# TensorE's queue kept in the order of the source from the third group on, and attention two slots sooner

## The chip, the cores and the metric

The kernel runs on one core of a Trainium2 chip. The metric is the time of one execution on the device, in microseconds; shown is the median of three runs. One further execution was recorded by the hardware profiler, and all rows below come from it.

## What is computed

Three layers in a row, all with fp32 inputs and outputs: a gated linear attention, a gated feed-forward layer, and a layer of eight experts of which each token uses one.

```python
# attention: 4 sequences, 8 heads, 768 steps, head size 48
for t in range(S):
    state = alpha[:, :, t, :, None] * state + einsum('bhd,bhe->bhde', k[:, :, t], v[:, :, t])
    y[:, :, t] = einsum('bhd,bhde->bhe', q[:, :, t], state)
# feed-forward: 3072 tokens, 384 -> 1536 -> 384
xn = x / sqrt(mean(x * x, -1) + 1e-6) * rms_g
x = (silu(xn @ w_gate) * (xn @ w_val)) @ w_out
# experts: 8 of 384 -> 1024 -> 384, one for each token
e = argmax(x @ r_gate)
out = prob[e] * sigmoid(x @ r_ogate)[e] * (relu(x @ w1[e]) @ w2[e])
```

## The kernel before

**Tiles and groups.** The 3072 tokens are worked in 24 tiles of 128. Attention goes tile by tile, in chunks of a sequence; tiles 0 to 17 take the first three sequences in turn, tiles 18 to 23 the last one. The feed-forward layer takes three tiles at a time: a group, g = 0 to 7, of 384 tokens.

**Feed-forward.** The inner size 1536 is cut into 12 blocks j. For each block there are three slots: ps_g (nine matmuls with w_gate, line 595), ps_v (nine with w_val), and ps_o (nine with w_out, line 629, for the block before). Each is three matmuls of high and low parts for three pieces of the sum or three tiles. These are the large matmuls: 128 rows, 128 columns of weights, 384 or 400 columns streamed, in the type fp32r. Groups 0 and 1 run first in halves, as the weights still arrive: run s = 0 is group 0 with blocks 0 to 5, s = 1 is group 1 with the same blocks, s = 2 and 3 are the two groups with blocks 6 to 11. Groups 2 to 7 follow, each with all 12 blocks. The experts come behind group 7.

**Attention.** Each tile has five stages on TensorE, in plain fp32, which lie between the slots of an earlier group:
- ps_s (line 416): the scores, eight small matmuls. Their operands have 48 rows each, heads of even number in rows 0 to 47 and of odd number in rows 64 to 111. VectorE masks them into P.
- ps_k (436): k transposed. The last tile of a sequence has none.
- ps_y (447 and 451): q times the running state (the tile "wide", all 128 rows and columns; the first tile of a sequence has none), then P times v, with 64 columns of weights.
- ps_st (472): the addition to the state.
- ps_x (493): the result transposed. It becomes xh and xl, which the next group's ps_g reads.

The stages of group 2's tiles (6, 7 and 8) lie in the runs s = 2 and 3, and those of group g + 1 in group g. VectorE makes qT and kT ahead (lines 315 and 397).

**What sets the order.** The program issues a slot and then, when the function due says so, a stage. A scheduler of the language, which goes by a timing model of its own, then orders the instructions of each engine, and may move one ahead of others that stand before it in the source. The call keep_in_program_order pins an instruction behind everything issued before it on its engine; it is used in a few places by name (the function pace and the tables K0, K1 and K2). Each engine takes its queue strictly in the resulting order.

Of the kernel before, what the change touches and what calls it, by code (L numbers as in the profile page):

```python
# [42 lines left out]
    'RB': 9,  # L43
    'LEADG': 6,
    'NAT': 5,
    'PET': 8,
    'NO': 'arkq',
}
# [4 lines left out]
def gla_glu_moe_kernel(  # L53
# [16 lines left out]
    nc = tc.nc  # L70
    P = 128
    B, H, S, D = q.shape
# [4 lines left out]
    KD = DM // P  # L77
# [5 lines left out]
    GT = 3  # L83
# [77 lines left out]
    def weight(nm, j):  # L161

        end = j >= JM
        if (nm, end) not in wts:
            n = KF - JM if end else JM
            wts[nm, end] = wpool.tile([P, n, WO] if nm[1] == "o" else [P, KD, n * P], F32R,
                                      tag=nm + "e" * end, name=nm + "e" * end)
        t_ = wts[nm, end]
        j -= JM * end
        return t_[:, j, :] if nm[1] == "o" else t_[:, :, j * P:j * P + P]  # L170
# [33 lines left out]
    xT = {}  # L204
    SEATS = CFG['SEATS']
    spread = [True]
    junk = [psM.tile([P, 4, P], F32, tag='o2', name='junk')]
    paced = [CFG['K0']]

# [191 lines left out]
    def stages(t):  # L401
        b, c = place_of[t]
        first, final = c == 0, c == NCH - 1
        en, qT, kT = pre[t]
        Sc = state_of[b % BS]
        S_ = wide[0]
        rs = [slice(64 * hh, 64 * hh + D) for hh in range(2)]
        g, ti = divmod(t, GT)
        Pt = {}

        def score():
            ps = [bank([P, NP, P], "ps_s") for _ in range(2)]
            for p in range(NP):
                for hh in range(2):
                    r = slice(64 * hh, 64 * hh + D)
                    nc.tensor.matmul(ps[hh][:, p, :], lhsT=kT[r, p, :], rhs=qT[r, p, :], start=True, stop=True)  # L416

            def post():
                if not first:
                    nc.vector.tensor_tensor(out=Sc, in0=Sc, in1=en.to_broadcast([P, NP, D]), op=ALU.mult)  # L420
                    for hh in range(2):
                        nc.scalar.activation(S_[rs[hh], :, hh * D:hh * D + D], Sc[rs[hh]], AF.Copy)
                mb = mask.to_broadcast([P, NP, P])
                for hh in range(2):
                    Ph = seat_of(t, f"P{hh}", [P, NP, P])
                    pace(f'Ph{t}', nc.vector.tensor_tensor(out=Ph, in0=ps[hh], in1=mb, op=ALU.mult))
                    Pt[hh] = Ph
            return post
        yield score

        def ktr():
            if final:
                return None
            ps = bank([P, NP, P], "ps_k")
            for p in range(NP):
                nc.tensor.transpose(ps[:, p, :], kT[:, p, :], ident)  # L436
            kn = seat_of(t, "kn", [P, H, 64])
            nc.scalar.activation(kn, ps.rearrange("p a (h d) -> p (a h) d", h=2), AF.Copy)
            Pt["kn"] = kn
            return None  # L440
        yield ktr

        def outp():
            ps = bank([P, DM], "ps_y")
            if not first:
                for p in range(NP):
                    nc.tensor.matmul(ps[:, p * 2 * D:p * 2 * D + 2 * D], lhsT=qT[:, p, :], rhs=S_[:, p, :],  # L447
                                     start=(p == 0), stop=False, skip_group_check=True)
            for h in (0, 2, 4, 6, 1, 3, 5, 7):
                for u in (slice(0, 64), slice(64, P)):  # L450
                    nc.tensor.matmul(ps[u, h * D:h * D + D], lhsT=Pt[h % 2][:, h // 2, u], rhs=vt[t][:, h, :],  # L451
                                     start=first, stop=True, skip_group_check=True)

            def post():
                xn = seat_of(t, "xn", [P, DM])
                ss = att.tile([P, 1], F32, tag="ss", name="ss", bufs=2)
                pace(f'xs{t}', nc.scalar.activation(xn, ps, AF.Square, accum_out=ss))  # L457
                nc.gpsimd.tensor_scalar(out=ss, in0=ss, scalar1=1.0 / DM, scalar2=1e-6, op0=ALU.mult, op1=ALU.add)  # L458
                pace(f'ss{t}', nc.gpsimd.tensor_tensor(out=ss, in0=ss, in1=mhalf, op=ALU.pow))
                pace(f'xa{t}', nc.scalar.activation(xn, ps, AF.Copy, scale=ss[:, 0:1]))  # L460
                Pt["xn"] = xn
            return post
        yield outp

        def state():
            if final:
                return None
            kn = Pt["kn"]
            ps = bank([P, NP, D], "ps_st")
            for p in range(NP):  # L470
                for hh in range(2):
                    nc.tensor.matmul(ps[64 * hh:64 * hh + 64, p, :], lhsT=kn[:, 2 * p + hh, :],  # L472
                                     rhs=vt[t][:, 2 * p + hh, :], start=True, stop=True)

            def post():
                if first:
                    nc.scalar.activation(Sc, ps, AF.Copy)
                else:
                    nc.vector.tensor_tensor(out=Sc, in0=ps, in1=Sc, op=ALU.add)
            return post  # L480
        yield state

        def xtr():
            if t and t + 2 < NTILE:
                load_v(t + 2)
            if ti == 0:
                xT[g] = (act.tile([P, KD, G], F32R, tag="xh", name="xh"),
                         act.tile([P, KD, G], F32R, tag="xl", name="xl"))
            xh, xl = xT[g]
            xn = Pt["xn"]  # L490
            ps = bank([P, KD, P], "ps_x")
            for kc in range(KD):
                nc.tensor.transpose(ps[:, kc, :], xn[:, kc * P:kc * P + P], ident)  # L493
            sl = slice(ti * P, ti * P + P)

            def post():
                xf = xn.rearrange("p (a b) -> p a b", a=KD)
                for kc in range(KD):
                    pace(f'xg{t}', nc.scalar.activation(xf[:, kc, :], ps[:, kc, :], AF.Copy, scale=gT[:, kc:kc + 1]))
                pace(f'xh{t}', nc.scalar.activation(xh[:, :, sl], xf, AF.Copy))  # L500
                pace(f'xl{t}', nc.vector.tensor_tensor(out=xl[:, :, sl], in0=xf, in1=f(xh[:, :, sl]), op=ALU.subtract))
            return post
        yield xtr
# [87 lines left out]
    def mm3(ps, wh, wl, xh, xl):  # L591
        n = 0
        for kc in range(KD):
            for a_, b_ in ((wh, xh), (wh, xl), (wl, xh)):
                nc.tensor.matmul(ps, lhsT=a_[:, kc, :], rhs=b_[:, kc, :],  # L595
                                 start=(n == 0), stop=(n == 3 * KD - 1))
                n += 1

    def m_val(g, j):
# [21 lines left out]
    def m_out(s, j):  # L621
        g, j0, j1 = runs[s]
        if j == j0:
            obank[s] = [psM.tile([P, WO], F32, tag=f"o{i}", name="ps_o") for i in range(GT)]
        hh, hl, _ = hbuf.pop((g, j))
        for i in range(GT):
            sl = slice(i * P, i * P + P)
            for n, (a_, b_) in enumerate(((hh, "woh"), (hh, "wol"), (hl, "woh"))):
                nc.tensor.matmul(obank[s][i], lhsT=a_[:, sl], rhs=weight(b_, j),  # L629
                                 start=(j == j0 and n == 0), stop=(j == j1 - 1 and n == 2))  # L630

    rows = {}

# [55 lines left out]
    def route_b(g):  # L689
        oh, ohb, ohc, m8, og, se = rt.pop(g)  # L690
        R = rows[g]
        ps = psR[0].tile([P, GT + 1, E], F32, tag=psR[1], name="ps_r")
        nc.tensor.matmul(ps[:, 0:1, :], lhsT=tri_b, rhs=ohb[:, 0:1, :], start=True, stop=True)
        for i in range(1, GT):
            nc.tensor.matmul(ps[:, i, :], lhsT=tri_b, rhs=ohb[:, i, :], start=True, stop=False)
            nc.tensor.matmul(ps[:, i, :], lhsT=ones_b, rhs=ohc[:, i - 1, :], start=False, stop=True)
        nc.tensor.matmul(ps[:, GT, :], lhsT=ones_b, rhs=ohc[:, GT - 1, :], start=True, stop=True)
        bc = [P, GT, E]

        nc.vector.tensor_scalar(out=se, in0=se, scalar1=1e-9, scalar2=2.0, op0=ALU.add, op1=ALU.mult)  # L700
# [151 lines left out]
    def due(s, n):  # L852

        if s == 0:
            return done < GS and (n + 1 - AHEAD) * GS >= (done + 1) * (N - AHEAD - CFG['TS'])
        k_ = done - GS
        return (n + 1 + N * (s - 2)) * GS >= (k_ + 1) * 2 * N and k_ < GS and (k_ < NST - 1 or s >= CFG['XG'])

    for s in range(4):
        N = 3 * (runs[s][2] - runs[s][1])  # L860
        paced[0] = CFG['K2'] if s else CFG['K1']
        for n in range(N):
# [193 lines left out]

    for g in range(2, NG):
        last = g == NG - 1
        if last:
            psA.release()  # L1060
            att.release()
# [285 lines left out]
```

## Time and profile before

| | |
|---|---|
| median of three runs | 876.1 us (875.66 to 876.71) |
| profiled execution, its time | 880.26 us |
| its span on the core | 878.6 us |
| TensorE, matmuls | 856.1 us busy, 97% |
| TensorE, weight loads | 814.5 us busy, 93% |
| VectorE | 489.3 us busy, 56% |
| ScalarE | 326.0 us busy, 37% |
| GpSimd | 143.8 us busy, 16% |
| mean granted clock of TensorE | 0.99 |

The busy time of matmuls overlaps, since one starts before the one ahead has ended, so it says that TensorE is never idle, and not how fast it works. A matmul in fp32 leaves two records in the trace for one of the source, one in fp32r a single one.

### The profile page before, as it was taken

To read this page: it belongs to the slowest core of one execution; us is meant where nothing else is said; L and a number is where in the kernel's file an instruction comes from. 1 tells how busy PE (TensorE), PEld (TensorE's weight loads), DVE (VectorE), ACT (ScalarE), POOL (GpSimd) and SP (SyncE) were. 2 spreads that over 40 slices of the span, in tenths; PEclk is the share of its full clock that TensorE was granted. 3 is DMA by queue.
4 is the path that set the end of the run, shared out by engine and by line. 5 is a ranking of instruction groups with operands and counts; after the bars stand their busy time and mean duration, and the time that the engine had idled before them with its cause. 6 is when DMAs were issued, how large, how long until landed. Compare 5 with 4: busy or idle time off the path is not lost.

```text
span 878.6 us, 15655 instructions
## 1 busy us (share of the span) xinstructions
PE 856.1 (97%) x6042; PEld 814.5 (93%) x6042; DVE 489.3 (56%) x1108; ACT 326.0 (37%) x708; POOL 143.8 (16%) x204
## 2 busy tenths in 40 slices
PE   7999999999999999999999999999999999999994
PEld 6799999899999999999999999999988999999994
DVE  7899987576854656655665552244454443444330
ACT  1655554234333233332322333334234442445431
POOL 2001001001100100010010010013032343344331
PEclk8999999999999999999999999999999999999998
DMA  9855534493311222132231010023056164256510
GB/s 190 181 163 149 175 83 122 117 258 89 104 49 36 78 57 61 43 87 60 59 87 47 13 37 1 1 93 98 1 182 197 60 212 144 65 190 198 178 41 24
DMA packets 121660, 88.46 MB, mean 101 GB/s; under 512 B 58219, under 2 KB 116716, under 8 KB 121584
## 3 DMA queue, kind: packets, MB, share of 16 engines
q1 hardware_dynamic: 117120, 77.97, 33.4%
q0 software_dynamic: 4464, 9.48, 3.1%
q8 instruction: 48, 0.79, 0.4%
q14 instruction: 28, 0.23, 0.1%
HBM read 71.62 MB, written 16.07 MB: 100 GB/s over the span
## 4 chain that ended last, share of the span: by engine, by line
PE 85%; DMA 5%; issue 4%; DVE 2%; POOL 1%; ACT 1%; SPq 1%; POOLq 0%; DVEq 0%; ACTq 0%
PE ps_o L629 18%; PE ps_v L595 18%; PE ps_g L595 18%; PE ps_b L1037 8%; PE ps_h L595 7%; PE ps_s L416 4%; PE ps_y L451 3%; DMA st<-in_moe_w_dram 3%; PE ps_y L447 2%; DMA er<-bucket 1%; PE ps_st L472 1%; PE ps_k L436 1%; PE ps_x L493 1%; POOL out_dram L1053 1%; PE pc L560 1%
## 5 line engine op out<-in xcount | busy, mean ns | idle before, releaser
L606 DVE TENSOR_TENSOR tt<-tt,ps_v 128x384 f32<-128x384 f32 x96 | 52.8, 550 | 140.9 <-PE ps_v L595 136.5
L587 ACT ACTIVATE tt<-ps_g 128x384 f32<-128x384 f32 x96 | 47.0, 490 | 135.4 <-PE ps_g L595 132.3
L609 ACT ACTIVATE hh<-tt 128x384 fp32r<-128x384 f32 x96 | 50.2, 523 | 119.6 <-DVE tt L606 119.2
L615 DVE TENSOR_TENSOR hl<-tt,hh 128x384 fp32r<-128x384 f32 x96 | 54.4, 567 | 28.1 <-ACT hh L609 27.4
L1037 PE MATMUL ps_b<-w2a,h 128*128 128x384 f32 (+2 forms) x336 | 67.4, 339 | 1.1 <-ACT h L1021 1.1
L595 PE MATMUL ps_g<-xh,wgh 128*128 128x384 f32 x192 | 68.1, 355 | 0.0
L595 PE MATMUL ps_v<-xh,wvh 128*128 128x384 f32 x192 | 68.0, 354 | 0.0
L1022 DVE SCALAR_TENSOR_TENSOR h<-ps_h,h 128x256 fp32r<-128x256 f32 (+6 forms) x72 | 38.0, 531 | 52.3 <-ACT h L1021 52.0
L629 PE MATMUL ps_o<-wol,hh 128*128 128x400 f32 x192 | 66.6, 347 | 0.0
L629 PE MATMUL ps_o<-woh,hh 128*128 128x400 f32 x192 | 66.5, 353 | 0.0
L1037 PE MATMUL ps_b<-w2b,h 128*114 128x384 f32 (+3 forms) x336 | 65.0, 338 | 0.2 <-ACT h L1021 0.2
L595 PE MATMUL ps_g<-xh,wgl 128*128 128x384 f32 x192 | 65.1, 339 | 0.0
L595 PE MATMUL ps_v<-xh,wvl 128*128 128x384 f32 x192 | 65.0, 339 | 0.0
L595 PE MATMUL ps_g<-xl,wgh 128*128 128x384 f32 x192 | 64.9, 338 | 0.0
L629 PE MATMUL ps_o<-woh,hl 128*128 128x400 f32 x192 | 64.7, 346 | 0.0
L595 PE MATMUL ps_v<-xl,wvh 128*128 128x384 f32 x192 | 64.7, 337 | 0.0
L1037 PEld LDWEIGHTS ps_b<-w2a,h 128*128 128x128 f32 (+2 forms) x336 | 57.5, 181 | 2.6 <-ACT h L1021 2.0
L1037 PEld LDWEIGHTS ps_b<-w2b,h 128*114 128x114 f32 (+3 forms) x336 | 57.5, 175 | 2.1 <-ACT h L1021 0.6
L595 PE MATMUL ps_h<-x,w1b 128*128 128x456 f32 (+3 forms) x288 | 58.5, 344 | 0.3 <-DVE h L1022 0.2
L1021 ACT ACTIVATE h<-ps_h 128x256 fp32r<-128x256 f32 (+6 forms) x72 | 33.3, 467 | 64.8 <-PE ps_h L595 60.4
L595 PE MATMUL ps_h<-x,w1a 128*128 128x256 f32 (+3 forms) x288 | 53.5, 328 | 0.6 <-DVE h L1022 0.6
L458 POOL TENSOR_SCALAR ss<-ss 128x1 f32<-128x1 f32 x24 | 6.4, 266 | 281.0 <-ACT xn L457 276.1
(284 smaller groups left out, 1994.9 us busy)
## 6 DMA issues: line engine op xcount, KB each, us to landing
st<-in_moe_w_dram SPq DMA_DIRECT2D x64, 384.0 KB, 5.4
bucket<-zero SPq DMA_DIRECT2D x8, 772.0 KB, 6.2
stg<-in_moe_w_gate_dram SPq DMA_DIRECT2D x12, 384.0 KB, 3.9
stg<-in_moe_w_val_dram SPq DMA_DIRECT2D x12, 384.0 KB, 3.7
stg<-in_moe_w_out_dram SPq DMA_DIRECT2D x12, 384.0 KB, 3.0
v<-in_v_dram SPq DMA_DIRECT2D x23, 192.0 KB, 2.8
blk_a<-in_alpha_dram SPq DMA_DIRECT2D x32, 96.0 KB, 2.2
blk_k<-in_k_dram SPq DMA_DIRECT2D x32, 96.0 KB, 2.3
```

What stands on the lines that cost most here:

```text
L416: nc.tensor.matmul(ps[hh][:, p, :], lhsT=kT[r, p, :], rhs=qT[r, p, :], start=True, stop=True)
L447: nc.tensor.matmul(ps[:, p * 2 * D:p * 2 * D + 2 * D], lhsT=qT[:, p, :], rhs=S_[:, p, :], start=(p == 0), stop=False, skip_group_check=True)
L451: nc.tensor.matmul(ps[u, h * D:h * D + D], lhsT=Pt[h % 2][:, h // 2, u], rhs=vt[t][:, h, :], start=first, stop=True, skip_group_check=True)
L587: nc.scalar.activation(tt, ps, AF.Silu)
L595: nc.tensor.matmul(ps, lhsT=a_[:, kc, :], rhs=b_[:, kc, :], start=(n == 0), stop=(n == 3 * KD - 1))
L606: nc.vector.tensor_tensor(out=tt, in0=tt, in1=ps, op=ALU.mult)
L609: nc.scalar.activation(hh, tt, AF.Copy)
L615: nc.vector.tensor_tensor(out=hl, in0=tt, in1=f(hh), op=ALU.subtract)
L629: nc.tensor.matmul(obank[s][i], lhsT=a_[:, sl], rhs=weight(b_, j), start=(j == j0 and n == 0), stop=(j == j1 - 1 and n == 2))
L1021: nc.scalar.activation(hh[:, 0, :], ps, AF.Relu)
L1022: nc.vector.scalar_tensor_tensor(out=hh[:, 1, :], in0=ps, scalar=0.0, in1=f(hh[:, 0, :]), op0=ALU.max, op1=ALU.subtract)
L1037: ins = nc.tensor.matmul(ob2[u][i][0:r], lhsT=hh[:, a_, sl], rhs=we[p][b_][:, j, :], start=(j == 0 and m == 0), stop=(j == KF2 - 1 and m = ...
```

## The change

A switch named strict is added. While it is set, a new function seq pins TensorE's instructions of the feed-forward layer, of the five stages and of the routing in the order of the source. It is off in the four half runs (the number STRICT is 4, and s is 0 to 3), on for the groups 2 to 6, and off for the last. Beside this the number XO moves the condition for the stages of tiles 6 to 8 by two slots.

```diff
+    'XO': 2,
+    'STRICT': 4,
...
+    strict = [False]
+
+    def seq(ins):
+
+        if strict[0]:
+            tc.keep_in_program_order(ins)
...
-                    nc.tensor.matmul(ps[hh][:, p, :], lhsT=kT[r, p, :], rhs=qT[r, p, :], start=True, stop=True)
+                    seq(nc.tensor.matmul(ps[hh][:, p, :], lhsT=kT[r, p, :], rhs=qT[r, p, :], start=True, stop=True))
...
-        return (n + 1 + N * (s - 2)) * GS >= (k_ + 1) * 2 * N and k_ < GS and (k_ < NST - 1 or s >= CFG['XG'])
+        return (n + 1 + CFG['XO'] + N * (s - 2)) * GS >= (k_ + 1) * 2 * N and k_ < GS and (k_ < NST - 1 or s >= CFG['XG'])
 
     for s in range(4):
+        strict[0] = s >= CFG['STRICT']
...
     for g in range(2, NG):
         last = g == NG - 1
+        strict[0] = g + 2 >= CFG['STRICT'] and not last
```

The matmuls and transpositions of ps_k, ps_y, ps_st, ps_x, ps_g, ps_v, ps_o and of the routing (ps_r) are wrapped in seq in the same way.

TensorE's queue at the scores of tile 11, in group 2, before; the rows left out are the rest of nine ps_g, of nine ps_v and of nine ps_o:

```order
L493 MATMUL ps_x<-ident,xn 128x128 x3
...
L595 MATMUL ps_g<-xh,wgl 128x384
L416 MATMUL ps_s<-qT,kT 128x128
L595 MATMUL ps_v<-xh,wvh 128x384
...
L629 MATMUL ps_o<-woh,hl 128x400
L416 MATMUL ps_s<-qT,kT 128x128 x7
L595 MATMUL ps_g<-xh,wgh 128x384
```

And now, with the lines of the changed source, which are 9 or so higher:

```order
L502 MATMUL ps_x<-ident,xn 128x128 x3
...
L604 MATMUL ps_g<-xh,wgl 128x384
L604 MATMUL ps_v<-xh,wvh 128x384
...
L638 MATMUL ps_o<-woh,hl 128x400
L425 MATMUL ps_s<-qT,kT 128x128 x8
L604 MATMUL ps_g<-xh,wgh 128x384
```

The first of the eight score matmuls has gone from its place behind ps_g to the other seven. Twelve more of the tiles 11 to 23 differ in the same way, three of them with two matmuls in the first piece and one with two early pieces.

TensorE's queue at the scores of tile 8, in the run s = 3, before:

```order
L493 MATMUL ps_x<-ident,xn 128x128 x3
L595 MATMUL ps_g<-xh,wgle 128x384
L595 MATMUL ps_v<-xh,wvhe 128x384
...
L629 MATMUL ps_o<-wol,hh 128x400
L416 MATMUL ps_s<-qT,kT 128x128 x2
L629 MATMUL ps_o<-woh,hl 128x400 x3
L416 MATMUL ps_s<-qT,kT 128x128 x6
L595 MATMUL ps_g<-xh,wghe 128x384
```

And now:

```order
L502 MATMUL ps_x<-ident,xn 128x128 x3
L604 MATMUL ps_g<-xh,wgle 128x384
L425 MATMUL ps_s<-qT,kT 128x128 x8
L604 MATMUL ps_v<-xh,wvhe 128x384
...
L638 MATMUL ps_o<-woh,hl 128x400
L445 MATMUL ps_k<-ident,kT 128x128 x4
L604 MATMUL ps_g<-xh,wghe 128x384
```

All eight now stand ahead of the nine ps_v, and the transposition of k, which came after the next ps_g and ps_v, ahead of that ps_g.

TensorE's queue at ps_y of tile 18, the first of the last sequence, before; the rows left out are nine ps_g and nine ps_v:

```order
L451 MATMUL ps_y<-v,P_4829 64x48
L595 MATMUL ps_g<-xh,wgh 128x384
...
L451 MATMUL ps_y<-v,P_4829 64x48
L595 MATMUL ps_v<-xh,wvh 128x384
...
L451 MATMUL ps_y<-v,P_4829 64x48 x6
L451 MATMUL ps_y<-v,P_4831 64x48 x8
L629 MATMUL ps_o<-wohe,hh 128x400
```

And now:

```order
L638 MATMUL ps_o<-wohe,hl 128x400
L604 MATMUL ps_g<-xh,wgh 128x384
...
L604 MATMUL ps_v<-xh,wvl 128x384
L460 MATMUL ps_y<-v,P_4829 64x48 x8
L460 MATMUL ps_y<-v,P_4831 64x48 x8
L638 MATMUL ps_o<-wohe,hh 128x400
```

The two early matmuls have joined the others behind ps_v.

## Rows read from the trace of the kernel before

**Rows 1.** Busy time of each engine in two stretches (us; records in brackets).
```profile
core 0: us, PE busy (x) PEld busy (x) DVE busy (x) ACT busy (x) POOL busy (x), PEclk, DMA share, GB/s
200.00:550.00 350.00, 350.00 (x2640) 331.45 (x2638) 201.92 (x480) 113.79 (x272) 31.13 (x59) 1.00 0.22 56
550.00:860.00 310.00, 307.14 (x1839) 298.83 (x1839) 126.40 (x259) 121.17 (x222) 94.63 (x65) 1.00 0.37 118
```

**Rows 2.** TensorE in order of time, first piece of tile 11: start, duration.
```profile
241.30 0.34 PE L595 MATMUL ps_g<-xh,wgh 128*128 128x384 f32 x1
...
242.18 0.34 PE L595 MATMUL ps_g<-xh,wgl 128*128 128x384 f32 x1
242.45 0.48 PE L416 MATMUL ps_s<-qT,kT 48*128 48x128 f32 x2
...
243.14 0.34 PE L595 MATMUL ps_v<-xl,wvh 128*128 128x384 f32 x1
```

**Rows 3.** The same view, the second piece of tile 11.
```profile
245.84 0.35 PE L629 MATMUL ps_o<-wol,hh 128*128 128x400 f32 x1
246.03 0.34 PE L629 MATMUL ps_o<-woh,hl 128*128 128x400 f32 x1
246.30 1.16 PE L416 MATMUL ps_s<-qT,kT 48*128 48x128 f32 x14
...
247.67 0.34 PE L595 MATMUL ps_g<-xl,wgh 128*128 128x384 f32 x1
```

**Rows 4.** The same view, the two pieces of tile 13.
```profile
291.90 0.49 PE L416 MATMUL ps_s<-qT,kT 48*128 48x128 f32 x4
...
292.60 0.34 PE L595 MATMUL ps_v<-xl,wvh 128*128 128x384 f32 x1
...
295.76 0.94 PE L416 MATMUL ps_s<-qT,kT 48*128 48x128 f32 x12
...
296.91 0.34 PE L595 MATMUL ps_g<-xl,wgh 128*128 128x384 f32 x1
```

**Rows 5.** The same view, tile 10, whose scores stand whole, with ps_r behind.
```profile
222.67 0.34 PE L595 MATMUL ps_g<-xh,wgl 128*128 128x384 f32 x1
222.94 1.16 PE L416 MATMUL ps_s<-qT,kT 48*128 48x128 f32 x16
224.04 0.18 PE L693 MATMUL ps_r<-ohb,tri_b 128*128 128x8 bf16 x1
...
224.20 0.42 PE L595 MATMUL ps_v<-xh,wvh 128*128 128x384 f32 x1
224.46 0.34 PE L595 MATMUL ps_v<-xl,wvh 128*128 128x384 f32 x1
```

**Rows 6.** Waits of the weight loads, 205 to 560 us: total, times, longest.
```profile
PEld ps_s L416 <- issue: 7.0, 28, 0.3
```

**Rows 7.** TensorE in order of time, two pieces of ps_y with the state.
```profile
190.55 0.34 PE L595 MATMUL ps_g<-xh,wgle 128*128 128x384 f32 x1
190.72 0.36 PE L447 MATMUL ps_y<-wide,qT 128*128 128x96 f32 x2
...
191.12 0.33 PE L595 MATMUL ps_v<-xl,wvhe 128*128 128x384 f32 x1
...
303.80 0.58 PE L447 MATMUL ps_y<-wide,qT 128*128 128x96 f32 x4
...
304.42 0.34 PE L595 MATMUL ps_v<-xl,wvh 128*128 128x384 f32 x1
```

**Rows 8.** The same view, ps_y of tile 18.
```profile
424.88 0.32 PE L451 MATMUL ps_y<-v,P 128*64 128x48 f32 x2
...
425.41 0.34 PE L595 MATMUL ps_v<-xl,wvh 128*128 128x384 f32 x1
...
426.91 1.02 PE L451 MATMUL ps_y<-v,P 128*64 128x48 f32 x28
```

**Rows 9.** VectorE in order of time: masks of tile 8, qT of tile 10.
```profile
186.03 1.26 DVE L426 TENSOR_TENSOR P<-ps_s,mask 128x512 f32<-128x512 f32 x2
...
218.66 0.69 DVE L397 TENSOR_TENSOR qT<-qT,aT 128x512 f32<-128x512 f32 x1
```

More of the change, by code (lines that the diff above doesn't have):

```diff
@@ L435, in ktr @@
             for p in range(NP):
-                nc.tensor.transpose(ps[:, p, :], kT[:, p, :], ident)
+                seq(nc.tensor.transpose(ps[:, p, :], kT[:, p, :], ident))
             kn = seat_of(t, "kn", [P, H, 64])
@@ L446, in outp @@
                 for p in range(NP):
-                    nc.tensor.matmul(ps[:, p * 2 * D:p * 2 * D + 2 * D], lhsT=qT[:, p, :], rhs=S_[:, p, :],
-                                     start=(p == 0), stop=False, skip_group_check=True)
+                    seq(nc.tensor.matmul(ps[:, p * 2 * D:p * 2 * D + 2 * D], lhsT=qT[:, p, :], rhs=S_[:, p, :],
+                                     start=(p == 0), stop=False, skip_group_check=True))
             for h in (0, 2, 4, 6, 1, 3, 5, 7):
                 for u in (slice(0, 64), slice(64, P)):
-                    nc.tensor.matmul(ps[u, h * D:h * D + D], lhsT=Pt[h % 2][:, h // 2, u], rhs=vt[t][:, h, :],
-                                     start=first, stop=True, skip_group_check=True)
+                    seq(nc.tensor.matmul(ps[u, h * D:h * D + D], lhsT=Pt[h % 2][:, h // 2, u], rhs=vt[t][:, h, :],
+                                     start=first, stop=True, skip_group_check=True))
             def post():
@@ L471, in state @@
                 for hh in range(2):
-                    nc.tensor.matmul(ps[64 * hh:64 * hh + 64, p, :], lhsT=kn[:, 2 * p + hh, :],
-                                     rhs=vt[t][:, 2 * p + hh, :], start=True, stop=True)
+                    seq(nc.tensor.matmul(ps[64 * hh:64 * hh + 64, p, :], lhsT=kn[:, 2 * p + hh, :],
+                                     rhs=vt[t][:, 2 * p + hh, :], start=True, stop=True))
             def post():
@@ L492, in xtr @@
             for kc in range(KD):
-                nc.tensor.transpose(ps[:, kc, :], xn[:, kc * P:kc * P + P], ident)
+                seq(nc.tensor.transpose(ps[:, kc, :], xn[:, kc * P:kc * P + P], ident))
             sl = slice(ti * P, ti * P + P)
@@ L594, in mm3 @@
             for a_, b_ in ((wh, xh), (wh, xl), (wl, xh)):
-                nc.tensor.matmul(ps, lhsT=a_[:, kc, :], rhs=b_[:, kc, :],
-                                 start=(n == 0), stop=(n == 3 * KD - 1))
+                seq(nc.tensor.matmul(ps, lhsT=a_[:, kc, :], rhs=b_[:, kc, :],
+                                 start=(n == 0), stop=(n == 3 * KD - 1)))
                 n += 1
@@ L628, in m_out @@
             for n, (a_, b_) in enumerate(((hh, "woh"), (hh, "wol"), (hl, "woh"))):
-                nc.tensor.matmul(obank[s][i], lhsT=a_[:, sl], rhs=weight(b_, j),
-                                 start=(j == j0 and n == 0), stop=(j == j1 - 1 and n == 2))
+                seq(nc.tensor.matmul(obank[s][i], lhsT=a_[:, sl], rhs=weight(b_, j),
+                                 start=(j == j0 and n == 0), stop=(j == j1 - 1 and n == 2)))
     rows = {}
@@ L692, in route_b @@
         ps = psR[0].tile([P, GT + 1, E], F32, tag=psR[1], name="ps_r")
-        nc.tensor.matmul(ps[:, 0:1, :], lhsT=tri_b, rhs=ohb[:, 0:1, :], start=True, stop=True)
+        seq(nc.tensor.matmul(ps[:, 0:1, :], lhsT=tri_b, rhs=ohb[:, 0:1, :], start=True, stop=True))
         for i in range(1, GT):
-            nc.tensor.matmul(ps[:, i, :], lhsT=tri_b, rhs=ohb[:, i, :], start=True, stop=False)
-            nc.tensor.matmul(ps[:, i, :], lhsT=ones_b, rhs=ohc[:, i - 1, :], start=False, stop=True)
-        nc.tensor.matmul(ps[:, GT, :], lhsT=ones_b, rhs=ohc[:, GT - 1, :], start=True, stop=True)
+            seq(nc.tensor.matmul(ps[:, i, :], lhsT=tri_b, rhs=ohb[:, i, :], start=True, stop=False))
+            seq(nc.tensor.matmul(ps[:, i, :], lhsT=ones_b, rhs=ohc[:, i - 1, :], start=False, stop=True))
+        seq(nc.tensor.matmul(ps[:, GT, :], lhsT=ones_b, rhs=ohc[:, GT - 1, :], start=True, stop=True))
         bc = [P, GT, E]
```

## Prediction

> **What bounds the kernel now.** I first read the busy time of the engines by stretch [rows 1]. From 200 to 550 us TensorE shows 350.00 us of matmul in 350 us, and the list of waits of its matmuls is empty from 205 to 560 us; VectorE has 202 us of work and ScalarE 114. From 550 to 860 us TensorE is still at 307 of 310. So this kernel lasts as long as TensorE's queue takes to run through, and only two things can move it: how much time the instructions of that queue take in the array, and gaps between them. A busy figure of 100% hides the first, because the end of a matmul is modelled and matmuls overlap. What counts is the distance from one start to the next, so the second view is the order of time on TensorE alone, read by starts.
>
> There the large matmuls of the feed-forward part follow each other very evenly: five intervals from 241.30 to 242.18, 0.176 us each [rows 2]; ps_o, with 400 columns, takes 0.19 [rows 3]. Between them lie the small groups of attention. The price of a group is the start of the last large matmul ahead of it to the start of the second one behind it, less two ordinary intervals. (The first one behind starts early enough but holds the next one up, so it must be inside.) An fp32 matmul of the source leaves two records, so the x8 of a ps_s in the program is x16 in the trace.
>
> The price of ps_s, whose operands have 48 of 128 rows:
> - one matmul alone (x2): 242.18 to 243.14 is 0.96, less 0.35: 0.61 us [rows 2]
> - two alone (x4): 291.90 to 292.60 is 0.70, with the same 0.27 ahead of it, less 0.35: 0.62 us [rows 4]
> - six (x12): 1.15 + 0.27 - 0.36 = 1.06 us [rows 4]
> - seven (x14): 246.03 to 247.67 is 1.64, less 0.36: 1.28 us [rows 3]
> - all eight (x16): 222.67 to 224.46 is 1.79, less 0.35 and the 0.16 of the six little ps_r behind it: 1.28 us [rows 5]
>
> The reader should see two things. The two halves of the array (the heads hh = 0 and 1) run side by side, so one matmul costs as much as two, and seven as much as eight; a pair more costs 0.22. And every piece pays about 0.40 for its two borders, whatever is in it: one pair alone is 0.62, not 0.22. The weight loads show the border itself: from 205 to 560 us they sat idle ahead of ps_s for 7.0 us in 28 places, 0.25 us each [rows 6].
>
> **The change, part by part.** With the order of the source kept, the scheduler can no longer send the first matmuls of a group ahead. On TensorE the rows of the program that differ are almost all of one kind: a group that stood in two or three pieces, nine or eighteen large matmuls apart, stands in one, at the place of the last piece.
>
> Pieces of ps_s in the third to seventh group of the feed-forward part (tiles 11 to 23, counted in the order of time of before, first pieces at 242.45 to 536.23 us):
> - nine tiles are cut into one and seven: 0.61 + 1.28 becomes 1.28, so 0.61 each, 5.49 us [rows 2, 3, 5]
> - three are cut into two and six: 0.62 + 1.06 becomes 1.28, 0.40 each, 1.20 us [rows 4, 5]
> - one is cut into one, one and six: 0.61 + 0.61 + 1.06 becomes 1.28: 1.00 us
>
> That is 7.69 us. The uncertain price is that of the whole group, since every place where it stands whole has something beside it. Its bounds: 1.28 as above, or 1.44 if the 0.16 is left inside, which takes 13 x 0.16 = 2.1 us off the sum. I take 1.28, because seven matmuls fill the same four pairs and were measured clean at 1.28.
>
> Pieces of ps_y. In most tiles the product with the running state (line 447, all 128 rows and columns) was cut too. This costs nothing: x2 alone is 190.55 to 191.12 less 0.35, 0.22 us, and x4 alone 303.80 to 304.42 with 0.17 ahead, less 0.35, 0.44 us [rows 7]. The price is proportional to the matmuls, with no border, as the shape is that of the large ones. So not the cutting as such is dear, but the change of the array's shape. Tile 18 is the exception: it begins a sequence and has no such product, so the part of line 451 with 64 columns is cut, into one, one and fourteen. One alone costs 0.53 + 0.27 - 0.35 = 0.45 us; inside the long run two records take 2 x 1.02/28 = 0.07 us [rows 8]. Joined up this gives 2 x (0.45 - 0.07) = 0.76 us. The cuts of ps_x at tile 15 keep the full shape and count nothing.
>
> The two slots. Tiles 6 and 7 come out in the old order, since the scheduler had already moved them as far as it wanted; tile 7 stays in six pieces. Tile 8 is what moves: its ps_s stands whole, fifteen large matmuls sooner, where it was cut into two and six: 0.40 us. I cost the move itself at nothing. Its masks (1.26 us on VectorE [rows 9]) are followed by eighteen large matmuls, 3.2 us, before ps_y; and the transposition ps_x of tile 8 now has eighteen large matmuls, again 3.2 us, ahead of the first ps_g that needs its result. If that cover fails, I put the loss at most at the 1.26 us of the masks, once.
>
> What is put in order elsewhere. At tile 10 ps_s goes ahead of nine ps_g, from 222.94 to about 221.3. Its qT is written from 218.66, 0.69 us long, so 2 us are left [rows 9]. No other group is asked for sooner than its last piece was, so no operand is late that was in time before, and the waits behind it (mask, norm, transposition) start from the end of the last piece as they did. VectorE and ScalarE get small exchanges of neighbours; they have 148 and 236 us to spare in those 350 [rows 1]. On SyncE's queue two loads of k stand a few places sooner and the clearing of one expert's bucket later; TensorE waits for no transfer in this stretch. The order pins instructions by place in the queue and adds no wait.
>
> Sum: 7.69 + 0.76 + 0.40 = 8.85 us off TensorE between 180 and 550 us. The last group and the experts (everything after 560 us) keep their order, and what they wait for, routing, gathered rows and expert weights, is released by work ahead of them, so they move up as a block. The profiled execution took 880.26 us, 4.2 more than the median of the plain runs; it would take 871.4. The same 8.85 off 876.1 gives 867.3 us.
>
> **A rule against it.** The weight loads stand still for 0.25 us ahead of each of the 28 pieces [rows 6]. The Trainium skill, TensorE: Matmul & The Clock Gate, Part 3 "The mechanism", says that the queue pulls a weight load ahead of running matmuls when it goes to other rows or to the background buffer. By that rule a lone piece would have its weights in place and pay no border. By it the sum would be that of the first rival below. This trace disagrees at these places.
>
> **The rivals.**
> Borders are not what is saved. If a piece cost only its pairs, at 0.22 (the difference between eight, 1.28, and six, 1.06, is that of one pair), the cuts into one and seven would give back one pair each, ten in all, 2.2 us, and nothing else: 873.9 us. Against it speaks that x2 was measured at 0.61. A milder form, in which the whole group keeps a cost that the pieces carried (1.44 and a stall of the masks at tile 8), gives 8.85 - 2.1 - 1.3 = 5.5 us, 870.6.
>
> No change: TensorE is through sooner and then waits in the experts for their weights, which come by transfers. Then it stays at 876. Against it: TensorE's 307 busy of 310 after 550 us leave 2.9 us of waiting in all, and these transfers are started by buffers that TensorE itself frees.
>
> Slower: in a fixed queue one late operand stops everything behind it, where the scheduler could have put other work first. The place would be each tile's ps_y, with its mask or its copy of the state late. There are 15 tiles in the fixed stretch, so at 0.59 us per tile the gain is used up; at 0.8 it is 15 x 0.8 - 8.85 = 3.2 us slower, 879.3. Against it: in before the last piece stood in the same place, behind the same matmuls, and the waits of TensorE's matmuls there are empty. The scheduler's early pieces filled no gap; they lay between matmuls that were not waiting.
>
> **How the numbers follow.** Chances: the forecast 0.80 (867.3, its own range 866.0 to 869.0), borders smaller than read or partly kept 0.10 (870 to 874), no change 0.04, slower 0.06. A measurement of this kernel, whose three runs lie within 0.12%, can tell about 0.2% (1.8 us) from no change; the second case lies outside that nearly always. So faster 0.90, same 0.04, slower 0.06. The range goes down to 865.5, half a microsecond beyond the forecast's own, for pieces whose price I took from one place, and up to 871.0 for the whole group at 1.44 with a stall at tile 8.
>
> **What would show it.** Right: weight loads idle ahead of ps_s in about 14 places in that stretch instead of 28, with the same 0.25 us; every ps_s from tile 8 on one x16 with a price near 1.28; large matmuls still 0.176 apart; the end of the seventh group some 8 us sooner, and everything after it sooner by the same amount. Wrong: matmuls of ps_y, ps_g or ps_k with waits on VectorE or ScalarE between 180 and 560 us; an x16 dearer than 1.44; or a gain at 560 us that has shrunk at 860, which would be the experts' transfers.

## The result, and the profile after

The changed kernel takes 867.58 us (median of five runs, 866.29 to 870.7), against 876.71 for the kernel before in the same measurement. The ratio is 0.9897, with a 95% interval of 0.987 to 0.9924: faster by 1.0%. Forecast were 867.3 us.

The profiled executions differ by more, 865.0 against 878.6 us of span, and this has to be taken apart first. Of the 13.6 us, 3.2 lie at the start, 9.0 in the stretch that the change touches, and 1.4 behind it. For the start, this is the busy time by stretch of the kernel before; PEclk is the granted clock of TensorE as a share of full speed:

```profile
10.00:20.00 10.00, 9.68 (x84) 8.48 (x86) 9.00 (x21) 1.57 (x4) 0.86 (x3) 0.74 1.27 246
```

And the same view of the kernel after:

```profile
10.00:20.00 10.00, 9.96 (x121) 8.25 (x120) 9.93 (x22) 2.38 (x8) 0.86 (x3) 1.00 1.26 246
```

In the profiled execution of before the granted clock was 0.74 in this stretch and 0.75 in the next one, so half of the time at the lower of its two levels, and the first ps_g came at 38.77 us in place of 35.56. This is no effect of the change: the queues are the same there, and two profiled executions of one and the same kernel (e8 and e11 below) differ in the same way, 38.83 against 35.62 us. Of the five runs of the changed kernel, those with a mean clock of 0.995 or more took 866.3 to 867.6, the two with 0.991 and 0.989 took 869.2 and 870.7.

So the measure below is the stretch from the first ps_g to the first matmul of the experts, ps_h. It leaves out the start and the experts, and holds all that was changed. Its two ends before, in order of time:

```profile
38.77 0.44 PE L595 MATMUL ps_g<-xh,wgh 128*128 128x384 f32 x1
...
625.55 0.40 PE L595 MATMUL ps_h<-x2a,w1a 128*128 128x256 f32 x2
```

and after:

```profile
35.56 0.44 PE L604 MATMUL ps_g<-xh,wgh 128*128 128x384 f32 x1
...
613.33 0.40 PE L604 MATMUL ps_h<-x2a,w1a 128*128 128x256 f32 x2
```

625.55 - 38.77 = 586.78 us became 577.77: 9.01 us less, where 8.85 were forecast. A second profile of the changed kernel gave 577.80 (e10), and the two of e8 and e11 differ by 0.07, while the times of the five runs lie 4.4 us apart. The gain comes tile by tile: counted from the first ps_g, the same matmul of ps_v starts as before up to 128 us, 0.95 us sooner at 206 us, 4.9 at 352, and 9.0 from 499 us on.

Inside it TensorE is as full as before [rows 1], and gets through more of its queue in the same time:

```profile
core 0: us, PE busy (x) PEld busy (x) DVE busy (x) ACT busy (x) POOL busy (x), PEclk, DMA share, GB/s
200.00:550.00 350.00, 350.00 (x2714) 336.96 (x2715) 204.78 (x483) 118.00 (x279) 30.90 (x61) 1.00 0.22 56
```

In the same 350 us run 2714 matmul records in place of 2640. The scores of tile 11, which lay in two pieces [rows 2, 3], in order of time:

```profile
241.87 0.34 PE L638 MATMUL ps_o<-woh,hl 128*128 128x400 f32 x1
242.14 1.16 PE L425 MATMUL ps_s<-qT,kT 48*128 48x128 f32 x16
243.23 0.45 PE L604 MATMUL ps_g<-xh,wgh 128*128 128x384 f32 x1
243.51 0.34 PE L604 MATMUL ps_g<-xl,wgh 128*128 128x384 f32 x1
```

The price of the whole group is 243.51 - 241.87 - 0.36 = 1.28 us, the value that was taken for it. And the waits of the weight loads ahead of ps_s (total, times, longest), from 195 to 550 us, which holds the scores of tiles 9 to 23:

```profile
PEld ps_s L425 <- issue: 3.9, 15, 0.3
```

15 places for 15 tiles, still 0.26 us each, where 205 to 560 us had 28 for 14 tiles [rows 6].

### The profile page after: what moved, and what is told of

Read it like the earlier page. It is cut to its first block, busy times and chain, and to the rows that moved or that the text cites. A ratio compares the mean times of both kernels' runs of the same rounds, so it can differ in the third digit from the quotient of the medians.

```text
span 865.0 us, 15658 instructions
## 1 busy us (share of the span) xinstructions
PE 842.6 (97%) x6042; PEld 808.0 (93%) x6042; DVE 490.6 (57%) x1108; ACT 327.5 (38%) x708; POOL 142.2 (16%) x204
## 4 chain that ended last, share of the span: by engine, by line
PE 86%; issue 4%; DMA 3%; DVE 3%; POOL 1%; ACT 1%; SPq 0%; POOLq 0%; DVEq 0%; ACTq 0%
PE ps_o L638 19%; PE ps_g L604 18%; PE ps_v L604 18%; PE ps_b L1047 9%; PE ps_h L604 9%; PE ps_s L425 3%; PE ps_y L460 3%; PE ps_y L456 2%; DMA st<-in_moe_w_dram 2%; DMA er<-bucket 1%; PE ps_st L481 1%; PE ps_k L445 1%; PE ps_x L502 1%; POOL out_dram L1063 1%; PE ps_t L1011 1%
## 5 line engine op out<-in xcount | busy, mean ns | idle before, releaser
L604 PEld LDWEIGHTS ps_h<-x,w1b 128*128 128x128 f32 x288 | 50.3, 188 | 1.2
```

The lines of the kernel that those rows point to most:

```text
L604: seq(nc.tensor.matmul(ps, lhsT=a_[:, kc, :], rhs=b_[:, kc, :], start=(n == 0), stop=(n == 3 * KD - 1)))
```

## The experiments

The theory: what is saved are the borders of the pieces, which cost because the array changes its shape, that is, the number of its rows or columns that a matmul uses. The rivals: that any cut into the large matmuls costs, whatever its shape; and that attention being sooner is what saves.

Each ratio is to the kernel before, timed beside the run on the same chip. The medians of different rows come from different chips, so the ratio and the stretch are what compares.

| run | median, us | ratio to before (interval) | first ps_g to ps_h, us |
|---|---|---|---|
| before | | 1 | 586.78 |
| changed | 867.58 | 0.9897 (0.987 to 0.9924) | 577.77 |
| e1, order alone | 872.38 | 0.9938 (0.9917 to 0.9959) | 581.97 |
| e2, sooner alone | 877.83 | 1.0 (0.9981 to 1.0019) | 586.78 |
| e3, all but the scores | 878.57 | 0.9999 (0.9983 to 1.0014) | 585.93 |
| e4, scores alone | 869.36 | 0.9913 (0.9883 to 0.9944) | 578.63 |
| e5, full rows, order of before | 875.33 | 0.9965 (0.9947 to 0.9982) | 584.14 |
| e6, full rows, new order | 873.98 | 0.9945 (0.9927 to 0.9964) | 582.92 |
| e7, heads apart | 879.45 | 1.0014 (1.0 to 1.0028) | 588.25 |
| e8, from the fourth run | 868.38 | 0.9878 (0.9858 to 0.9898) | 575.28 |
| e9, one slot | 870.63 | 0.991 (0.9885 to 0.9934) | 578.95 |
| e10, changed again | 868.68 | 0.9892 (0.9867 to 0.9918) | 577.80 |
| e11, from the fourth run again | 867.5 | 0.9876 (0.9848 to 0.9904) | 575.35 |
| e12, from the first run | 876.2 | 0.9982 (0.9959 to 1.0004) | 585.27 |

**e1: the fixed order without the two slots.**

```diff
-    'XO': 2,
+    'XO': 0,
```

> The fixed order alone, with the stages of tiles 6 to 8 where they were. If what is saved are the borders of the pieces of ps_s (theory), all of it is here but the 0.40 us of tile 8, whose scores stay cut into two and six: 8.45 us less than before, about 868.2. If the gain came from attention being two slots sooner (rival), nothing is left: 876.7. In the trace: 15 or 16 idle places of the weight loads ahead of ps_s from tile 9 on become one for each tile.

Only 4.81 of the 8.45 us came in the stretch. TensorE in order of time, at the start of group 2; the brackets hold the idle time ahead and what ended it:

```profile
198.74 0.49 PE L502 MATMUL ps_x<-ident,xn 128*128 128x128 f32 x3
200.81 0.44 PE L604 MATMUL ps_g<-xh,wgh 128*128 128x384 f32 x1 [1.59 <-ACT xh L509]
201.41 0.44 PE L604 MATMUL ps_g<-xl,wgh 128*128 128x384 f32 x1 [0.15 <-DVE xl L510]
...
202.57 0.52 PE L604 MATMUL ps_g<-xh,wgl 128*128 128x384 f32 x1
202.89 0.52 PE L604 MATMUL ps_g<-xh,wgh 128*128 128x384 f32 x1
...
203.98 1.71 PE L425 MATMUL ps_s<-qT,kT 48*128 48x128 f32 x16
205.63 0.44 PE L604 MATMUL ps_v<-xh,wvh 128*128 128x384 f32 x1
```

The first ps_g of group 2 needs the transposed tile 8, whose ps_x stands right ahead of it in the source. Before, the scheduler put the scores of tile 9, nine ps_o and ps_k between, 3.62 us from ps_x to ps_g:

```profile
201.43 0.49 PE L493 MATMUL ps_x<-ident,xn 128*128 128x128 f32 x3
201.85 1.16 PE L416 MATMUL ps_s<-qT,kT 48*128 48x128 f32 x16
...
204.70 0.60 PE L436 MATMUL ps_k<-ident,kT 128*128 128x128 f32 x4
205.05 0.42 PE L595 MATMUL ps_g<-xh,wgh 128*128 128x384 f32 x1
```

In the fixed order nothing lies between, and TensorE waits 1.59 + 0.15 = 1.74 us. Then the matmuls are 0.32 us apart and not 0.175, which the granted clock explains (busy time by stretch, the clock third from the end):

```profile
200.00:202.00 2.00, 1.03 (x4) 0.78 (x5) 0.56 (x1) 0.73 (x2) 0.00 (x0) 0.94 0.00 0
202.00:204.00 2.00, 2.00 (x9) 1.56 (x7) 0.00 (x0) 0.00 (x0) 0.00 (x0) 0.50 0.00 0
204.00:206.00 2.00, 2.00 (x19) 1.88 (x19) 0.27 (x1) 0.49 (x1) 0.00 (x0) 0.71 0.00 0
```

By these shares it is at the lower of its levels, 1.2 GHz, from about 201.8 to about 205.2 us. The 4.20 us that this run is behind the changed kernel are 0.40 for tile 8's pieces, 1.74 of waiting and 2.06 that are left. Of these the rows show 1.6 for the clock: seven ps_g of 0.145 too much, and ps_s at 1.65 in place of 1.09. The other 0.5 were not traced. In the changed kernel the same ps_x has eighteen large matmuls behind it:

```profile
194.63 0.49 PE L502 MATMUL ps_x<-ident,xn 128*128 128x128 f32 x3
...
198.17 0.34 PE L604 MATMUL ps_g<-xh,wgh 128*128 128x384 f32 x1
198.34 0.34 PE L604 MATMUL ps_g<-xl,wgh 128*128 128x384 f32 x1
```

No wait. So the two slots, worth 0.40 us by the prediction, are what lets the fixed order pay in full: without them 4.20 of its 9.01 us are lost.

**e2: the two slots without the fixed order.**

```diff
-    'STRICT': 4,
+    'STRICT': 99,
```

> The two slots alone, the scheduler free as before. Tile 8's scores stand whole (0.40 us saved), but those of tile 9, whole before, are now cut into six and two (0.62 + 1.06 in place of 1.28, 0.40 lost), and tiles 11 to 23 keep their pieces. Theory: no change, 876.7. Rival (attention sooner is what saves): about 867.6.

The stretch is 586.78 us, to the hundredth that of before, and the time is the same. By themselves the two slots give nothing, so the rival that attention sooner saves time is out.

**e3 and e4: one kind of matmul pinned at a time.** In e3 seq is taken off the scores, in e4 off everything else.

```diff
-                    seq(nc.tensor.matmul(ps[hh][:, p, :], lhsT=kT[r, p, :], rhs=qT[r, p, :], start=True, stop=True))
+                    nc.tensor.matmul(ps[hh][:, p, :], lhsT=kT[r, p, :], rhs=qT[r, p, :], start=True, stop=True)
```

> The whole change, but the matmuls of ps_s are not pinned; the order then has the pieces of ps_s as before (tile 8 whole, tile 9 cut), while all of ps_y is joined up. Theory (a border costs because the shape of the array changes): only tile 18's ps_y is saved, 0.76 us: 875.9, within the noise of before. Rival (any cut into the run of large matmuls costs, whatever the shape; some twenty cuts of ps_y and fifteen of ps_s share the 9 us): about 5 us less, 871.4.

> Only the matmuls of ps_s are pinned (and the two slots kept); ps_y stays cut as before, in tile 18 too. Theory: 7.69 + 0.40 = 8.1 us less than before, 868.6, as the twenty cuts of ps_y with the state cost nothing. Rival (any cut costs): 3.6 us less, 873.1.

e3 is 0.85 us shorter in the stretch and not to be told from before in time; e4 is 8.15 shorter. The sum is 9.00. So the cuts of ps_y with the state, which e3 joins up, cost nothing, and nearly the whole 9 us were the cuts of ps_s. The scheduler cut them a little differently in e3, tiles 11 to 23 in twelve places into one and seven and in one into two and six, at the same price by the list: 12 x 0.61 + 0.40 = 7.72 us in place of 7.69.

**e5 and e6: the scores in the shape of the large matmuls.** The decisive pair. The order of the queues is that of before and that of the change; only the rows of the operands differ, so that the scores are those of both heads of a pair, summed.

```diff
-                    nc.tensor.matmul(ps[hh][:, p, :], lhsT=kT[r, p, :], rhs=qT[r, p, :], start=True, stop=True)
+                    nc.tensor.matmul(ps[hh][:, p, :], lhsT=kT[:, p, :], rhs=qT[:, p, :], start=True, stop=True)
```

> The kernel before, in the same order, but each matmul of ps_s takes all 128 rows of kT and qT instead of 48, so that both heads of a pair are summed in its scores (part of the computation is changed: later values and the choice of experts differ, and with them perhaps the time behind 560 us). The shape of the array is then that of the large matmuls. Theory: the pieces have no border and cost by their matmuls alone, an estimate of 0.22 to 0.25 each from ps_y with 96 columns, so one alone (x2) falls from 0.61 to 0.25, and the pieces of a tile sum to the same 1.8 to 2.0 us as a whole group. Rival (cutting itself costs): one alone stays at 0.6 or more. Between 200 and 560 us the idle places of the weight loads ahead of ps_s vanish by the theory, stay 28 by the rival.

> The same change of the scores on top of the changed kernel, in its order (again the scores of both heads of a pair are summed). Theory: with no borders there is nothing to save but tile 18's ps_y, so the stretch from the scores of tile 9 to the end of attention is 0.8 us shorter than in the run with the order of before, and the times differ by about 0.1%. Rival (cutting itself costs): about 8 us shorter, as in the original pair.

A first piece in e5:

```profile
262.47 0.34 PE L595 MATMUL ps_g<-xh,wgle 128*128 128x384 f32 x1
262.64 0.38 PE L416 MATMUL ps_s<-qT,kT 128*128 128x128 f32 x2
...
263.04 0.34 PE L595 MATMUL ps_v<-xl,wvhe 128*128 128x384 f32 x1
```

263.04 - 262.47 - 0.35 = 0.22 us, where the same piece with 48 rows cost 0.61. And a whole group in e6:

```profile
241.46 0.34 PE L638 MATMUL ps_o<-woh,hl 128*128 128x400 f32 x1
241.64 1.95 PE L425 MATMUL ps_s<-qT,kT 128*128 128x128 f32 x16
...
243.60 0.33 PE L604 MATMUL ps_g<-xl,wgh 128*128 128x384 f32 x1
```

243.60 - 241.46 - 0.35 = 1.79 us, eight times 0.22. In neither of the two does the list of waits of the weight loads from 205 to 560 us have a line of ps_s any more. The stretches differ by 1.22 us, not by 9. Of this 0.22 stand already at the third microsecond of the stretch, where the queues are the same, and 0.8, from 0.37 to 1.15, comes in at tile 18, where 0.8 was expected. So the same cuts in the same places cost nothing once the shape stays: the rival that cutting itself costs is out, and the border is the change of shape.

e5 shows one thing more. With all 128 rows each of the eight matmuls takes 0.22 us, 1.79 us for a tile, where a whole group with four pairs side by side took 1.28. Yet its stretch is below before's (584.14 against 586.78), because in that order the borders weigh more than the lost pairing: the six pieces of tile 7 alone cost 6 x 0.61 = 3.7 us before.

**e7: the heads apart.**

```diff
-            for p in range(NP):
-                for hh in range(2):
+            for hh in range(2):
+                for p in range(NP):
                     r = slice(64 * hh, 64 * hh + D)
```

> The changed kernel with the two loops of ps_s exchanged: the four matmuls of the even heads first, then the four of the odd heads, so that neighbours use the same rows of the array. Theory (two halves of the array work side by side, a pair costs 0.22): up to eight turns in place of four, 1.28 becomes as much as 2.16 us, 0.88 for each of 24 tiles, 21 us slower than the changed kernel, about 888. If the pairing of neighbours is not what makes x2 cost as much as x4: 1.28 and 867.6.

```profile
244.53 0.34 PE L638 MATMUL ps_o<-woh,hl 128*128 128x400 f32 x1
244.80 1.71 PE L425 MATMUL ps_s<-qT,kT 48*128 48x128 f32 x16
246.44 0.44 PE L604 MATMUL ps_g<-xh,wgh 128*128 128x384 f32 x1
246.72 0.33 PE L604 MATMUL ps_g<-xl,wgh 128*128 128x384 f32 x1
```

246.72 - 244.53 - 0.35 = 1.84 us in place of 1.28, and the stretch is 10.5 us longer than the changed kernel's, where 21 were expected for the whole kernel. Pairing is real, but worth less than was read into it, 0.56 us for a group and not 0.88: less the 0.40 of the borders, eight turns take 1.44, 0.18 each, and four pairs 0.88, 0.22 each. Two neighbours in different halves overlap for the most part, and eight of one half are a little quicker each than a pair.

**e8 and e11: the fixed order from the fourth half run on.**

```diff
-    'STRICT': 4,
+    'STRICT': 3,
```

> The changed kernel with the fixed order one run sooner (STRICT 3, so from the run s = 3 on). The scores of tile 7, six pieces in both kernels, stand whole. Theory: six prices of 0.61 become 1.28, 2.4 us less than the changed kernel: 865.2. Rival (there the scheduler's freedom hides something, as the last weights are still being converted): a wait of TensorE appears in this stretch, and the time is 867.6 or more.

> The fixed order from the run s = 3 on, beside the changed kernel on the same chip. Its first trace had the stretch from the first ps_g to the experts at 575.3, 2.5 less than the changed kernel, but its time was no lower, with the clock at half for longer at the start. Theory (six pieces of tile 7 joined are 2.4 us): 0.28% below the changed kernel in time. Rival (given back behind): equal to it.

The six pieces of tile 7 are one group, no matmul waits that did not wait before, and the stretch is 575.28 and 575.35 us: 2.5 below the changed kernel (2.4 expected). The medians beside each other on one chip are 867.5 (e11) and 868.7 (e10, the changed kernel); the intervals overlap, so by the median alone this is a tie. The two profiled executions, in which the first ps_g starts at nearly the same time (35.62 and 35.73 us), took 865.54 and 868.50 us. So the traces say that it is the better one, and that nothing of it is given back behind.

**e9: one slot.**

```diff
-    'XO': 2,
+    'XO': 1,
```

> The changed kernel with attention of tiles 6 to 8 one slot sooner in place of two. In the run with none, ps_g of group 2 stood right behind tile 8's transposition: TensorE waited 1.59 and 0.15 us for xh and xl (first ps_g 2.07 us after the start of ps_x, the one with xl 2.67 after), then ran at half clock for some 3 us, 1.7 to 2 us more. Here nine ps_o stand between, 0.33 + 1.64 us. Theory (the slots serve to cover ps_x to xl): a wait of 0.1 to 0.6 us, no fall of the clock, and a stretch from the first ps_g to the first matmul of the experts of about 578.2 us, 0.4 more than the changed kernel and 3.8 less than with none. Rival (each slot is worth half): 579.9.

> The changed kernel itself, as the measure for the three others on this chip: about 0.990 of before; the stretch from the first ps_g to the first matmul of the experts 577.8 us.

```profile
196.78 0.49 PE L502 MATMUL ps_x<-ident,xn 128*128 128x128 f32 x3
199.13 0.44 PE L604 MATMUL ps_g<-xh,wgh 128*128 128x384 f32 x1 [0.22 <-ACT xh L509]
199.78 0.45 PE L604 MATMUL ps_g<-xl,wgh 128*128 128x384 f32 x1 [0.21 <-DVE xl L510]
```

Nine ps_o between leave two small waits, and the clock stays at 1.00. The stretch is 578.95: 1.15 us more than the changed kernel beside it (e10), where 0.4 was expected. The two waits are 0.43 of it; around them the matmuls also lose their overlap (the first two ps_g are 0.65 apart and not 0.175). The first slot is worth 3.0 us, the second 1.15.

**e12: the fixed order from the first half run on.**

```diff
-    'STRICT': 4,
+    'STRICT': 0,
```

> The fixed order from the run s = 0 on. The scores of tiles 4 and 5, two pieces each in the changed kernel, stand whole too; two pieces of two pairs at 0.84 become 1.28, 0.40 for each tile, 0.8 us below the run from s = 3 if no operand is late. Rival (in the first two runs the weights still arrive, and the scheduler's freedom covers that): TensorE waits there, and if a wait is over a microsecond the clock may fall as in the run without the two slots; a few microseconds slower than from s = 3.

```profile
46.41 0.84 PE L569 MATMUL pc<-wr,wT 128*128 128x16 f32 x6 [2.77 <-ACT xn L469]
...
118.71 0.34 PE L604 MATMUL ps_v<-xh,wvl 128*128 128x384 f32 x1
121.99 0.52 PE L561 MATMUL pt<-ident,Fo 128*128 128x128 f32 x3 [2.94 <-DVE Fo L530]
122.26 0.47 PE L638 MATMUL ps_o<-woh,hh 128*128 128x400 f32 x1
122.53 0.54 PE L638 MATMUL ps_o<-wol,hh 128*128 128x400 f32 x1
122.86 0.54 PE L638 MATMUL ps_o<-woh,hl 128*128 128x400 f32 x1
```

The stretch is 585.27 us, 9.9 longer than from the fourth run on, and nearly the whole gain is gone. In the first runs TensorE also transposes the weights that VectorE converts (Fo). In a fixed queue one such transposition stops the nine ps_o behind it for 2.94 us, and the clock falls again (0.63 from 122 to 124 us, 0.52 from 124 to 126): the ps_o behind are 0.33 us apart. From the last ps_v ahead to the next ps_g, at 126.13 us, it takes 7.42 us, 4.7 more than the same stretch one block earlier (2.73). It is not the only place. A wait of 2.77 us for ScalarE ends at 46.41 us, with the clock at 0.50 from 48 to 50 us, and two shorter waits, of 0.80 and 0.73 us, end at 40.60 and 57.91 us. This is the slower rival, at another place than the prediction had put it.

## Why the prediction was right

- The price list: one piece of ps_s 0.61, a whole group 1.28, borders about 0.40, cuts of ps_y with the state free. All of it stood: the whole group was measured at 1.28 or 1.29 in all of tiles 9 to 23, e4 gave 8.15 of 8.1 us, e3 0.85 of 0.76, and e5 with e6 showed that it is the shape.
- The choice of 1.28 over 1.44 for the whole group: right; the 0.16 belonged to ps_r.
- The sum: 8.85 forecast, 9.01 measured in the stretch, 9.13 in the medians.
- The tail moves up as a block: from ps_h to the end it is 253.0 us before and 251.7 after. That it is shorter is no effect of the change, as the second profile of the changed kernel has 253.3 there.
- The loads still stand idle 0.26 us ahead of each group, and the gain is not the 2.2 us that free borders would have left. So the rule of the Trainium skill (TensorE: Matmul & The Clock Gate, Part 3 "The mechanism") that the queue pulls weight loads ahead does not hold at these places. Where the shape stays (e5, e6) no such wait is left.
- The step that was mis-sized is the two slots. They were costed as 0.40 us for tile 8 and a move at nothing, and if the cover failed, a loss of 1.26 us at most. Alone they are worth 0.00 (e2, since tile 9 is cut in exchange), and beside the fixed order 4.2 (e1): without the cover the loss is 3.8 us beside the 0.40, three times that bound. The sum came out right because it was made for both edits together, with the cover of 3.2 us ahead of ps_g named and present; what that cover is worth, and that the scheduler had provided it by other means, was not seen. To that extent the hit is luck. "The scheduler's early pieces filled no gap" is true of the pieces of ps_s and ps_y that were joined here, from tile 11 on. At the start of group 2 and in the first half runs its reordering did cover waits (e1, e12).
- The slower rival has a real mechanism. Its place is not ps_y, where no run showed a wait, but the first ps_g of group 2 (e1) and, in the first half runs, the work on the weights (e12).

## What to carry to other kernels

On a full TensorE, count the borders between matmuls of different array shape, and keep those of one shape together: here each interruption cost about 0.40 us, and cuts among matmuls of the same shape were free. Read prices from start to second next start, since a busy time of 100% shows none of this. A fixed order pays where nothing is late, and takes away the cover that a scheduler gave where something is: look for the first consumer behind each transposition, and move the producer far enough ahead in the source before pinning.

## What was not expected of the hardware

A wait of 1.74 us (e1) was followed by some 3 us with TensorE at the lower level of its clock, and cost 3.8 us in all; one of 2.94 us (e12) was followed by about as long a stretch, and cost 4.7. Waits of 0.22 and 0.21 us (e9) left it at full speed, and so did one of 2.19 us among the experts in the second profile of the changed kernel (e10), where the granted clock is 1.00 from 650 to 658 us:

```profile
651.81 0.97 PE L1047 MATMUL ps_b<-w2a,h 128*128 128x384 f32 x4 [2.19 <-ACT h L1031]
```

So the length of a wait alone does not say whether the clock falls. What else decides was not tried.
